# Reordering the first stage of a planned attention and feed-forward kernel: due times of its own for each of the first twelve f-tiles

## The chip, the cores and the metric

The kernel runs on one core of one Trainium2 chip. The metric is device time in microseconds of one execution; the median of several runs counts. Engines are named as in the profile: PE is TensorE, PEld its weight loads, DVE is VectorE, ACT is ScalarE, POOL is GpSimd, SP is SyncE, which issues most of the transfers.

## What is computed

Eight batches of eight heads of attention over 576 tokens with a head width of 64, and a feed-forward block of width 2048 on the result:

```python
scores = (q @ k.T) / sqrt(64)          # heads 0-3: only the last 32 keys
                                       # heads 4-7: only keys at a distance that is a multiple of 32
attn = exp(scores - max); attn /= sum(attn) + 1e-9
x = (attn @ v), heads side by side     # 4608 tokens x 512
h = x @ w_in                           # 512 x 2048
g = h * erf(softplus(h))
out = g @ w_out                        # 2048 x 512, float32
```

## The kernel before

**The work.** A pair of heads is one unit of attention; batch b has the pairs 0 to 3, and a name such as `qk_0_2` or `s_2_0` carries batch and pair. A pair goes through loads of qk and v, scores (PE), maximum, difference, exp and sum (DVE and ACT), the norm (POOL), a transposition, the product with v (PE), and a split of the result into a rounded part `xhi` (ACT, line 543) and a rest `xlo` (DVE, line 548). Batches 0 and 1 are written by `heads` (PE transposes, lines 505 and 524); batches 2 to 7 by `Pair` and `burst`, where one PE burst holds the product of one pair and the scores of the next (lines 649 and 669).

**Weights.** The feed-forward weights come as 64-bit words in sixteen tiles of 1 MB: w0 to w7 are pieces of `w_in`, w8 to w15 of `w_out`. `weight` unpacks each on DVE with three instructions (`bits0`, `bits1`, `bits2`, lines 849, 856, 862), rounds it on ACT (`split_hi`, line 867) and takes the rest on DVE (`split_lo_w`, line 870); the result is the tile `pair`.

**f-tiles.** `ftile` number k works on 128 columns of the hidden layer for 512 tokens of a batch: mm1 is twelve matmuls into a bank h or c (line 900); softplus and erf on ACT (lines 908, 911); the product on DVE (914); a rounded part `ghi` on ACT (917) and a rest `glo` on DVE (920); mm2 is twelve matmuls into the banks o0 to o3 (line 953). Two consecutive f-tiles share a tile of each weight. There are 144. Of the first, k = 0 to 3 are columns 0 to 3 of batch 0, k = 4 to 9 columns 0 to 5 of batch 1, k = 10 to 21 the others of batch 0. From k = 16 on mm1 uses the bank h alone, and a copy on DVE (`hs`, line 905) empties it.

**What sets the order.** Nothing is ordered by hand. `Plan` takes every step with an engine, an estimated duration, the steps it waits for and a due time, and lays the steps out one by one; the program is then written in that order, which each engine and each queue keeps. The due times are numbers in tables: KP for the attention pairs, KW for the unpacking of weights and KL for their loads, KI for the identity matrix, and FT for an f-tile: `at(i)` adds FT[i] to `PRO + SLOT * k` for softplus, erf, product, ghi, glo and mm2. `stash` stores the last 64 tokens of x on SP's queue for a chunk that is done at the end. Where PE would have nothing to do, the plan puts in a filler, a matmul of constants into a free bank (`warm`, line 1111), up to the mm1 of f-tile 6. `stay` (line 748) is four copies on POOL in a `Pair`; `PAIRS` says which banks and which weight tiles' room the pairs of batches 0 and 1 use.

Of the kernel before, what the change touches and what calls it, by code (L numbers as in the profile page):

```python
# [18 lines left out]
P = 128  # L19
# [9 lines left out]
PRO = 32  # L29
SLOT = 6.1  # L30
BACKLOG = 1.1130116
FT = (-2658.81, -1917.57, -3180.58, -1587.7, 370.28, 2216.13)
KI = -5711.28
KW = (
    (515.126, 145.354, -2348.96, -944.277, 1286.67, 3206.16, 5188.84, 898.14),
    (3223.92, 1696.94, 1126.17, 225.88, 917.373, 2507.48, 968.087, 687.694),
)
KL = (
    (1396.48, 770.086, 437.181, 1627.04, 1025.57, 3014.12, 4245.01, 2397.07),
    (945.031, -1252, 3215.3, 3000.01, 1806.83, 496.124, 738.615, -241.399),  # L40
)
KP = (
    (542.197, -1847.5, -1823.21, -1021.52, -228.67, -599.586, 241.152),
    (-276.384, -1335.88, 230.421, 74.7754, 61.6955, 1875.1, 500.521),
    (-3437.85, -358.658, -2301.53, -516.546, -1428.1, -1124.22, -1341.66),
    (-681.281, -64.094, -3.54274, 242.205, 753.958, -909.211, 891.395),
    (295.78, 1348.87, -519.101, -887.072, -1312.65, -1072.32, 546.505),
    (2178.78, -52.1175, 1285.12, 2385.15, -1099.07, 1937.66, 1486.77),
    (229.525, -1120.81, -1531.76, 458.111, -1237.4, 1489.49, 2057.23),
    (797.817, 454.351, -1337.33, -438.439, 405.282, -2692.97, -46.1439),  # L50
    (-263.256, -1479.86, -803.403, -1222.11, -1640.52, -729.701, -1160.22),
    (-56.753, -688.408, -1119, -2398.06, -1589.54, -528.693, -1803.55),
    (1701.86, -255.027, -218.21, 579.17, -2586.31, 474.53, 1124.51),
    (-1172.45, -389.859, -1119.5, 318.434, -1231.62, -605.957, 902.288),
    (2032.67, -285.494, 2320.84, 2718.33, 797.304, 1224.77, 2105.28),
    (185.837, 739.768, -248.587, 1446.15, 465.44, -982.033, -1572.57),
    (2173.08, -714.7, -89.7886, 1415.69, -653.201, 472.77, 2089.39),
    (-2448.89, -2823.79, -164.701, -2885.72, -3171.85, -833.514, -516.643),
    (173.604, -1291.81, 1443.08, 358.408, 1375.5, 281.827, 532.185),
    (-860.33, 173.881, -1669.94, -1368.01, -1271.17, -59.054, 19.7547),  # L60
    (-535.718, 791.315, -703.505, 428.52, -239.186, 1515.88, -829.14),
    (384.84, 22.9069, 191.935, 6.45996, 1625.85, 711.713, -785.021),
    (528.925, 813.537, -227.9, 758.411, 1271.32, -177.238, -283.018),
    (-983.339, 288.565, -1751.94, -152.244, -1780.28, -2884.66, -147.489),
    (-636.401, 555.939, -914.57, -54.0228, -991.538, -550.356, -1882.44),
    (-16.9022, -1698.68, -2124.61, -849.243, -749.766, -1907.47, 43.8626),
    (-281.424, 1163.73, 2667.33, 323.962, 2162.26, 1855.22, 2704.8),
    (-852.152, 81.5048, 131.859, -85.8376, 448.274, 857.394, -841.094),
    (1090.46, -1203.43, -1500.89, -1488.65, -582.704, -1479.82, -2024.72),
    (-1250.03, -2543.42, -1893.9, -2382.58, 212.636, -378.546, -1317.93),  # L70
    (-268.103, -1245.63, 369.011, -959.82, -353.937, -241.546, -491.086),
    (1006.02, -817.882, -1149.69, -1072.6, -81.8383, 825.626, 339.559),
    (614.205, 1964.07, 594.824, 1636.03, -61.9141, -185.064, 2530.02),
    (-444.459, -1478.15, -205.633, -1936.09, -288.964, -2805.35, -2230.9),
)
PAIRS = (
    (("h", "c"), None, True, True),
    (("o0", "o1"), (2, 3), True, True),
    (None, (10, 11), False, True),
    (("o2", "o3"), (4, 5), True, True),  # L80
    (None, (12, 13), False, True),
    (("o0", "o1"), (6, 7), True, True),
    (("o2", "o3"), (14, 15), True, True),
    (None, None, False, True),
)
# [79 lines left out]
class Plan:  # L165
# [114 lines left out]
def attention_moe(  # L280
# [329 lines left out]
    class Pair:  # L610
# [72 lines left out]
        def soft(self):  # L683
            loc, units, add = self.loc, self.units, plan.add
            cols = 64 * units
            k_q, k_v, k_s, k_m, k_n, k_t, k_x = self.keys
            s, pid = self.s, self.pid
            sm = buf("apool", "sm", [P, 2, 384], f"sm_{pid}")
            tt = buf("apool", "sm", [P, 2, 384], f"tt_{pid}")
            pt = buf("apool", "sm", [P, 2, 64 * units], f"pt_{pid}")  # L690
# [59 lines left out]
            def exchange():  # L750
# [4 lines left out]
            n = 2 * cols  # L755
            o = add("dve", dve(n), k_m, mask, [self.o_s], [], [s])
            o = add("dve", dve(n), k_m + 0.05, maxi, [o], [mx], [s])
            o = add("dve", dve(n), k_m + 0.1, less, [o], [sm], [s, mx])
            o = add("act", act(n, 0.08), k_m + 0.1, exp, [o], [], [sm])
            o.table = "exp"  # L760
            o = add("dve", dve(n), k_n, total, [o], [rc], [sm])
            o = add("dve", 0.31, k_n + 0.05, invert, [o], [], [rc])
            o = add("pool", 0.1 + n / 500.0, k_n + 0.1, norm, [o], [], [sm, rc])
            o = o_t = add("dve", dve(n) + 0.07, k_t, flip, [o, *turn_of("t")], [tt], [sm])
            turns["t"] = o
            o = add("pool", 0.0, k_t + 0.1, claim, [o], [pt])
            self.ready = [
                add("pool", 4 * (0.06 + cols / 1000.0), k_t + 0.2, stay, [o], [], [tt, pt]),
                add("sp", 1.0, k_t + 0.2, exchange, [o], [], [tt, pt]),
            ]  # L770
            self.ready[1].issues = 4
# [114 lines left out]
    def ftile(k, c, f, first_f, last_f, ready):  # L886

        v0 = PRO + SLOT * k
# [33 lines left out]
        add = plan.add  # L922
        ta, tp, td = act(CH), act(CH, 0.05), dve(CH)

        def at(i):
            return FT[i] + v0

        first = add("pe", 2.73, v0, mm1, ready[0] + mm1_first[-1:], [ph])
        first.words = 24
        o = first  # L930
        if not early:
            o = add("dve", td, at(2), keep, [o], [hs], [ph])
        o = add("act", tp, at(0), softplus, [o] + gates[-1:] * (k % 2 == 0), [a], [hs])
# [11 lines left out]
        for t in range(NTT):  # L945
# [4 lines left out]
            def mm2(t=t, po=po):  # L950
# [14 lines left out]
            if f == last_f:  # L965
# [25 lines left out]
                if t % 2 == 0:  # L991
                    o = o_e = add("act", act(DM, 0.06), v0 + 2.5 * SLOT + 0.7 + 0.2 * t, evac, [o], [ob], [po])
                else:
                    eng, n = ("dve", dve(DM)) if c == B else ("act", act(DM, 0.06))
                    o = add(eng, n, v0 + 2.5 * SLOT + 0.7 + 0.2 * t, evac, [o, o_e], [], [po, ob])
# [6 lines left out]
                else:  # L1002
                    o = add("pool", 1.2, o.key + 0.1, accumulate, [o, stored[c, t]], [], [ob])
# [25 lines left out]
    mm1_of, mm1_first, hi_of, gates = {}, [], [], []  # L1029
# [38 lines left out]
    for b in range(B):  # L1068
        p2 = b // 2
        for i, hp in enumerate(ORDER if p2 else (0, 1, 2, 3)):  # L1070
            keys = KP[4 * b + i]
            if p2 == 0:
                banks, home, act_sum, pool_norm = PAIRS[4 * b + i]
                done, o_s, o, loads = heads(
                    b, hp, keys, [], pe_mask=True, pool_norm=pool_norm, act_sum=act_sum, banks=banks, home=home, own=True
                )
# [11 lines left out]
            if p2:  # L1088
                n = 4 * b + i + 1
# [15 lines left out]
            chunk(B, 0, NFC)  # L1105
    def warm(tag):
        n = len(plan.ops)
        w = buf("ps_a", "ps", [P, 2, 512], f"warm{n}") if tag == "ps" else buf("ps_o", tag, [P, 512], f"warm{n}")

        def run():  # L1110
            yield nc.tensor.matmul(w[:, 0, :] if tag == "ps" else w[:, :], ident_b, con[:, :512], start=True, stop=True)

        return w, run

    w, run = warm("o3")
    first = plan.add("pe", 0.217, -10.0, run, o_con, [w])
    plan.filler = (first, warm, ("o3", "o2", "o1", "o0", "ps"), mm1_first[6])
    for op in plan.order():
        for x in op.new:
            x.tile = x.make()  # L1120
# [104 lines left out]
```

## Time and profile before

| | us |
|---|---|
| median of 3 runs | 910.86 (910.26 to 910.88) |
| the profiled execution, its own time | 910.45 |
| its span, first to last instruction | 908.7 |
| PE busy in the span | 874.5 |
| ACT busy | 588.5 |
| DVE busy | 500.2 |
| POOL busy | 116.1 |

The profile's page gives each engine's busy time and, in 40 slices of 22.7 us, its busy share in tenths. The chain of work is followed back from the last instruction: what released each step. A row of a timeline is start and duration in us, engine, line, operation, tile written and tile read; a number at the end in brackets is the idle time before it and what ended it. A busy PE is not PE at its peak, since the ends of its pipelined matmuls are modelled.

### The profile page before, as it was taken

The page shows a single profiled execution, that of the slowest core. Times are in us where ns is not written, and L with a number is a line of the kernel's source. Part 1 is how long each engine was busy: PE and PEld are TensorE (multiplying, and loading weights), DVE is VectorE, ACT ScalarE, POOL GpSimd, SP SyncE. Part 2 cuts the span into 40 slices and gives each one's busy share as a digit, 9 for nine tenths or more (in the row PEclk, how much of TensorE's full clock was granted, in tenths as well). Part 3 has the DMA queues.
Part 4 walks back from the last instruction along what each step waited for, and adds up shares of the span by engine and source line. Part 5 has one row for each costly group of instructions (what it writes and reads, how often), then busy time and mean ns, then how long its engine had stood idle before and what let it go on. Part 6 is the DMA issues. An engine that isn't in the chain of part 4 may idle for free.

```text
span 908.7 us, 18092 instructions
## 1 busy us (share of the span) xinstructions
PE 874.5 (96%) x7425; PEld 718.4 (79%) x7427; DVE 500.2 (55%) x793; ACT 588.5 (65%) x880; POOL 116.1 (13%) x156
## 2 busy tenths in 40 slices
PE   3678999999999999999999999999999999999997
PEld 2567888888888888888888888888888888888886
DVE  4998893555655545555555556555555333333332
ACT  2795876657666666677777667666766665556553
POOL 1210200021121111111111211111111100000000
PEclk9898999999999999999999999999999999999999
DMA  9995110133242122311221123212321310001001
GB/s 355 350 392 168 53 47 1 46 90 71 85 102 72 53 67 81 99 55 55 64 89 59 42 70 103 70 58 69 103 70 30 96 47 1 1 1 47 1 1 46
DMA packets 37298, 75.24 MB, mean 83 GB/s; under 512 B 12960, under 2 KB 16288, under 8 KB 37216
## 3 DMA queue, kind: packets, MB, share of 16 engines
q1 hardware_dynamic: 34576, 69.24, 22.5%
q0 software_dynamic: 2400, 4.46, 2.5%
q8 instruction: 58, 0.95, 0.4%
q10 hardware_dynamic: 240, 0.39, 0.2%
q14 instruction: 24, 0.20, 0.1%
HBM read 56.12 MB, written 13.63 MB: 77 GB/s over the span
## 4 chain that ended last, share of the span: by engine, by line
PE 92%; DVE 4%; ACT 2%; DMA 1%; issue 1%; SPq 0%; POOL 0%; DVEq 0%; ACTq 0%; POOLq 0%
PE o L953 44%; PE h L900 42%; PE x L669 3%; PE s L649 2%; ACT v L470 1%; DMA con<-consts 1%; DVE pair L870 1%; PE s L524 0%; DVE mx L434 0%; DVE w L856 0%; DVE w L862 0%; DVE w L849 0%; PE s L505 0%; DVE xlo L548 0%; DVE a L914 0%
## 5 line engine op out<-in xcount | busy, mean ns | idle before, releaser
L953 PE MATMUL o<-pair,ghi 128*128 128x512 f32 x1152 | 359.8, 394 | 2.6 <-DVE xlo L548 2.6
L900 PE MATMUL h<-xhi,pair 128*128 128x512 f32 x1152 | 287.0, 391 | 2.3 <-DVE a L914 2.1
L900 PEld LDWEIGHTS h<-xhi,pair 128*128 128x128 f32 x1152 | 216.6, 189 | 49.2 <-DVE a L914 2.4
L953 PEld LDWEIGHTS o<-pair,ghi 128*128 128x128 f32 x1152 | 215.2, 189 | 48.1 <-DVE xlo L548 2.7
L953 PE MATMUL o<-pair,glo 128*128 128x512 f32 x576 | 224.9, 391 | 0.0
L905 DVE COPY hs<-h 128x512 f32<-128x512 f32 x128 | 88.0, 688 | 158.6 <-PE h L900 158.6
L917 ACT CAST ghi<-a 128x512 fp32r<-128x512 f32 x144 | 89.1, 620 | 132.9 <-PE o L953 121.0
L900 PE MATMUL h<-xlo,pair 128*128 128x512 f32 x576 | 154.0, 389 | 0.0
L908 ACT ACTIVATE a<-hs 128x512 f32<-128x512 f32 x128 | 80.9, 632 | 99.1 <-DVE hs L905 84.7
L914 DVE TENSOR_TENSOR a<-a,hs 128x512 f32<-128x512 f32 x128 | 85.3, 708 | 102.1 <-ACT a L911 102.0
L920 DVE TENSOR_TENSOR glo<-a,ghi 128x512 fp32r<-128x512 f32 x144 | 99.3, 692 | 59.0 <-ACT ghi L917 58.0
L953 PEld LDWEIGHTS o<-pair,glo 128*128 128x128 f32 x576 | 108.7, 189 | 22.9
L900 PEld LDWEIGHTS h<-xlo,pair 128*128 128x128 f32 x576 | 108.1, 188 | 22.5
L908 ACT ACT_TABLE_LOAD x79 | 101.4, 1283 | 21.2 <-DVE hs L905 17.7
L726 POOL TENSOR_TENSOR sm<-sm,r 128x640 f32<-128x640 f32 (+1 forms) x24 | 36.3, 1513 | 470.3 <-DVE r L723 451.8
L911 ACT ACT_TABLE_LOAD x72 | 92.4, 1283 | 1.3
L911 ACT ACTIVATE a<-a 128x512 f32<-128x512 f32 x144 | 83.2, 624 | 0.8
L748 POOL COPY pt<-tt 32x320 f32<-32x320 f32 (+1 forms) x96 | 53.1, 553 | 39.5 <-DVE tt L732 36.0
L706 DVE TENSOR_TENSOR s<-s,con 128x640 f32<-128x640 f32 (+1 forms) x24 | 21.6, 900 | 31.6 <-PE s L649 31.6
L974 ACT COPY ob<-o 128x512 f32<-128x512 f32 x42 | 24.2, 585 | 10.9 <-PE o L953 8.6
L669 PEld LDWEIGHTS x<-pt,v 64*64 64x64 f32 x1392 | 24.4, 134 | 8.5 <-issue 8.5
L715 ACT ACT_TABLE_LOAD x24 | 30.8, 1283 | 0.4
(66 smaller groups left out, 503.1 us busy)
## 6 DMA issues: line engine op xcount, KB each, us to landing
v<-v_loc SPq DMA_DIRECT2D x16, 640.0 KB, 5.8
qk<-qk_loc SPq DMA_DIRECT2D x16, 592.0 KB, 5.5
words<-w_out SPq DMA_DIRECT2D x8, 1024.0 KB, 7.8
words<-w_in SPq DMA_DIRECT2D x8, 1024.0 KB, 7.3
out<-ob SPq DMA_DIRECT2D x32, 256.0 KB, 2.2
qk<-qk_res SPq DMA_DIRECT2D x12, 656.0 KB, 4.4
v<-v_str SPq DMA_DIRECT2D x16, 384.0 KB, 3.9
qk<-qk_str SPq DMA_DIRECT2D x4, 608.0 KB, 7.1
```

Of the source, the lines that this page charges most:

```text
L669: yield nc.tensor.matmul(self.x[m][d, n * a : n * (a + 1)], self.v[rows, (2 * a + h) * D : (2 * a + h) * D + D], p, start=True, stop=True,)
L715: yield nc.scalar.activation(sm[:, :, :cols], sm[:, :, :cols], AF.Exp, scale=1.0 / D**0.5)
L726: yield nc.gpsimd.tensor_tensor(out=wide(sm), in0=wide(sm), in1=spread(rc), op=ALU.mult)
L748: yield nc.gpsimd.tensor_copy(pt[quarter(m, f), f, :], plane(m, f, f))
L900: yield nc.tensor.matmul(ph[:, :CH], win[f // 2][:, w, 2 * P * cc + f0 : 2 * P * cc + f0 + P], x[cc][:, c0 : c0 + CH], start=(i == 0), sto ...
L905: yield nc.vector.tensor_copy(hs.tile, ph.tile)
L908: yield nc.scalar.activation(a.tile, hs.tile, AF.Softplus)
L911: yield nc.scalar.activation(a.tile, a.tile, AF.Erf)
L914: yield nc.vector.tensor_tensor(out=a.tile, in0=a.tile, in1=hs.tile, op=ALU.mult)
L917: yield nc.scalar.copy(ghi.tile, a.tile)
L920: yield nc.vector.tensor_tensor(out=glo.tile, in0=a.tile, in1=ghi.tile.bitcast(F32), op=ALU.subtract)
L953: yield nc.tensor.matmul(po.tile, g[:, ts], wout[f // 2][:, w, f % 2 * SW : f % 2 * SW + SW], start=(f == first_f and i == 0), stop=(f == ...
```

## The change

No step is added to the attention or the feed-forward work and none is taken away. What changes is the numbers by which the plan orders them, and four small things:

- a new table FE gives each of the first twelve f-tiles six due times of its own; FT, now with other numbers, holds from the thirteenth on
- KI, KW, KL and KP have other numbers throughout
- the plan's estimate of `stay` is 0.95 + cols/320 instead of 4 * (0.06 + cols/1000)
- fillers may use the banks c and h too, and go on up to the mm1 of f-tile 8
- PAIRS is written on one line, with the same content

```diff
-FT = (-2658.81, -1917.57, -3180.58, -1587.7, 370.28, 2216.13)
-KI = -5711.28
+FT = (-1281.04, -3645.45, -2381.23, -1076.53, 664.202, 2244.2)
+FE = (
+    (1750.73, -78.9746, -156.706, 86.3883, 561.264, -292.723),
...
+)
+KI = -1253.92
...
-                add("pool", 4 * (0.06 + cols / 1000.0), k_t + 0.2, stay, [o], [], [tt, pt]),
+                add("pool", 0.95 + cols / 320.0, k_t + 0.2, stay, [o], [], [tt, pt]),
...
-            return FT[i] + v0
+            return (FE[k][i] if k < len(FE) else FT[i]) + v0
...
-        w = buf("ps_a", "ps", [P, 2, 512], f"warm{n}") if tag == "ps" else buf("ps_o", tag, [P, 512], f"warm{n}")
+        if tag == "ps":
+            w = buf("ps_a", "ps", [P, 2, 512], f"warm{n}")
+        else:
+            w = buf("ps_h" if tag in "hc" else "ps_o", tag, [P, 512], f"warm{n}")
...
-    plan.filler = (first, warm, ("o3", "o2", "o1", "o0", "ps"), mm1_first[6])
+    plan.filler = (first, warm, ("o3", "o2", "o1", "o0", "ps", "c", "h"), mm1_first[8])
```

The new lines move the code: line 849 of before is 856 after, 914 is 921, 706 is 713, and so on by 7 (the filler, 1111, by 10).

SP's queue at the program's start, before. `ident` and `con` are constants, `words9` is a weight tile, `qk` and `v` the inputs of a pair.

```order
L1013 DMA ident_87<-ident_f 128x128
L384 DMA qk_0_2_89<-qk_str 128x1216
L838 DMA words9_93<-w_out 128x2x1024
L384 DMA qk_0_3_95<-qk_str 128x1216
L387 DMA v_0_2_90<-v_str 128x768
L384 DMA qk_0_1_99<-qk_loc 128x1184
L1010 DMA con_85<-consts 128x576
L387 DMA v_0_3_96<-v_str 128x768
L384 DMA qk_1_2_108<-qk_str 128x1216
L384 DMA qk_1_0_113<-qk_loc 128x1184
L387 DMA v_0_1_100<-v_loc 128x1280
L387 DMA v_1_2_109<-v_str 128x768
```

The same place after.

```order
L391 DMA qk_0_0_87<-qk_loc 128x1184
L1020 DMA ident_90<-ident_f 128x128
L391 DMA qk_0_2_92<-qk_str 128x1216
L1017 DMA con_85<-consts 128x576
L391 DMA qk_0_1_96<-qk_loc 128x1184
L394 DMA v_0_0_99<-v_loc 128x1280
L394 DMA v_0_2_93<-v_str 128x768
L391 DMA qk_0_3_147<-qk_str 128x1216
L394 DMA v_0_1_97<-v_loc 128x1280
L845 DMA words8_240<-w_out 128x2x1024
L845 DMA words0_288<-w_in 128x4x512
L391 DMA qk_1_2_311<-qk_str 128x1216
```

The first weight goes from the third place to the tenth, the constants from the seventh to the fourth, pair 0 of batch 0 to the front.

DVE around the mask of `s_2_0`, its first instruction of batch 2, before. `w32` and `pair` are weight tiles being unpacked, `a` and `glo` belong to f-tiles.

```order
L849 TENSOR_SCALAR w32_15_1079<-words15_994 128x1024
L920 TENSOR_TENSOR glo_2_1085<-a_2_1004,ghi_2_1077 128x512
L548 TENSOR_TENSOR xlo3_84<-s_1_3_784,xhi3_80 128x18x18
L548 TENSOR_TENSOR xlo3_84<-s_1_3_784,xhi3_80 128x18x14
L856 SCALAR_TENSOR_TENSOR w32_15_1079<-words15_994,w32_15_1079 128x1024
L862 SCALAR_TENSOR_TENSOR w32_15_1079<-words15_994,w32_15_1079 128x1024
L706 TENSOR_TENSOR s_2_0_1098<-s_2_0_1098,con_85 128x2x320
```

The same place after.

```order
L856 TENSOR_SCALAR w32_2_1055<-words2_958 128x1024
L555 TENSOR_TENSOR xlo0_81<-s_1_0_859,xhi0_77 128x256
L555 TENSOR_TENSOR xlo0_81<-s_1_0_859,xhi0_77 128x320
L863 SCALAR_TENSOR_TENSOR w32_2_1055<-words2_958,w32_2_1055 128x1024
L869 SCALAR_TENSOR_TENSOR w32_2_1055<-words2_958,w32_2_1055 128x1024
L927 TENSOR_TENSOR glo_3_1127<-a_3_971,ghi_3_1124 128x512
L713 TENSOR_TENSOR s_2_0_1083<-s_2_0_1083,con_85 128x2x320
```

Before, the unpacking ahead of the mask covers w9, w1, w8, w0, w2, w3, w11, w7 and w15, the last two without `split_lo_w`; after it covers w8, w0, w1, w9, w4 and w2, again the last two without it. The mask is DVE's instruction 113 before (counted from 0, the branch at the start among them) and 101 after.

## Rows read from the trace of the kernel before

**Rows 1.** The page: busy us (share) xinstructions; below, busy tenths in 40 slices.

```profile
PE 874.5 (96%) x7425; PEld 718.4 (79%) x7427; DVE 500.2 (55%) x793; ACT 588.5 (65%) x880; POOL 116.1 (13%) x156
...
PE   3678999999999999999999999999999999999997
...
DVE  4998893555655545555555556555555333333332
```

**Rows 2.** The chain (start us, us, what), and PE's only wait after 84 us.

```profile
84.48 5.71 PE h L900 x24
...
152.78 2.72 PE h L900 x12
...
PE h L900 <- DVE hs L905: 0.2, 1, 0.2
```

**Rows 3.** Stretches: us, busy by engine (x instructions), PE's granted clock, DMA share, GB/s.

```profile
7.97:84.52 76.55, 54.38 (x1146) 41.95 (x1148) 67.69 (x112) 51.40 (x165) 13.79 (x13) 0.87 0.92 339
84.52:137.10 52.58, 52.58 (x232) 43.48 (x233) 46.84 (x56) 41.45 (x54) 5.01 (x5) 1.00 0.16 57
137.10:151.45 14.35, 14.35 (x65) 11.89 (x64) 4.58 (x8) 7.97 (x12) 0.00 (x0) 1.00 0.00 1
```

**Rows 4.** Timeline of DVE, the mask of `s_2_0`.

```profile
84.52 0.83 DVE L706 TENSOR_TENSOR s<-s,con 128x640 f32<-128x640 f32 x1
```

**Rows 5.** Unpacking on DVE, 7.97 to 84.52 us: ns min/median/max, first and last start.

```profile
L849 DVE TENSOR_SCALAR w<-words x9: 655/694/1954, 8.0 to 79.5; 128x1024 uint32<-128x1024 uint32 x9
L856 DVE SCALAR_TENSOR_TENSOR w<-words,w x9: 1209/1226/1773, 8.7 to 82.1; 128x1024 uint32<-128x1024 uint32 x9
L862 DVE SCALAR_TENSOR_TENSOR w<-words,w x9: 1211/1225/1744, 10.0 to 83.3; 128x1024 uint32<-128x1024 uint32 x9
L870 DVE TENSOR_TENSOR pair<-w,pair x7: 1185/1217/1226, 12.3 to 68.8; 128x1024 fp32r<-128x1024 f32 x7
```

**Rows 6.** The start: DVE's first instruction, the constants and PE in the chain, DVE's first reduce.

```profile
7.97 0.69 DVE L849 TENSOR_SCALAR w<-words 128x1024 uint32<-128x1024 uint32 x1 [7.97 <-DMA words<-w_out]
...
4.01 8.37 DMA con<-consts
12.43 0.82 PE s L411 x2
...
13.44 0.95 DVE L434 TENSOR_REDUCE mx<-s 128x12 f32<-128x768 f32 x1
```

**Rows 7.** Transfers issued by 24 us: queue, count, KB each, median us to landing.

```profile
qk<-qk_str SPq DMA_DIRECT2D x4, 608.0 KB, 7.1
words<-w_out SPq DMA_DIRECT2D x2, 1024.0 KB, 10.2
...
qk<-qk_loc SPq DMA_DIRECT2D x3, 592.0 KB, 10.9
v<-v_str SPq DMA_DIRECT2D x3, 384.0 KB, 8.8
...
con<-consts SPq DMA_DIRECT2D x1, 144.0 KB, 8.4
ident<-ident_f SPq DMA_DIRECT2D x1, 64.0 KB, 1.8
```

**Rows 8.** Stretches up to the landing of the constants, columns as in rows 3.

```profile
0.00:4.00 4.00, 0.00 (x0) 0.00 (x0) 0.00 (x0) 1.49 (x2) 0.30 (x5) 1.00 0.44 132
4.00:12.38 8.38, 1.56 (x48) 1.37 (x48) 3.23 (x4) 1.04 (x1) 0.00 (x0) 1.00 1.02 406
```

**Rows 9.** Timeline of PE, a filler.

```profile
37.37 0.63 PE L1111 MATMUL warm<-con 128*128 128x512 bf16 x1
```

**Rows 10.** Timeline of SP, the first store of rest tokens.

```profile
26.00 0.33 SPq L1051 DMA_DIRECT2D rests<-xhi  x1
```

**Rows 11.** Timeline of POOL and DVE, a norm and an unpacking step that it overlaps.

```profile
55.61 2.17 POOL L496 TENSOR_TENSOR v<-v,r 128x384 f32<-128x384 f32 x2 [5.70 <-DVE r L488]
...
57.09 1.77 DVE L856 SCALAR_TENSOR_TENSOR w<-words,w 128x1024 uint32<-128x1024 uint32 x1
```

More of the change, by code (lines that the diff above doesn't have):

```diff
@@ L31 @@
 BACKLOG = 1.1130116
-FT = (-2658.81, -1917.57, -3180.58, -1587.7, 370.28, 2216.13)
-KI = -5711.28
+FT = (-1281.04, -3645.45, -2381.23, -1076.53, 664.202, 2244.2)
+FE = (
+    (1750.73, -78.9746, -156.706, 86.3883, 561.264, -292.723),
+    (-1873.53, -1131.49, -3255.33, -1932.5, -68.3526, -2636.75),
+    (-440.156, 494.33, -2418.01, -324.007, -279.52, -1957.1),
+    (-2493.93, -2196.69, -1337.47, -2683.09, -1942.8, -740.706),
+    (-359.715, -339.561, -756.812, -395.038, -948.712, 554.973),
+    (-1263.5, 98.006, -351.554, -2365.23, -1954.63, -1761.8),
+    (-241.219, -1177.42, 1412.51, 536.763, 444.719, -1139.03),
+    (644.806, -259.744, 2143.44, 1710.4, 45.7892, -1067.48),
+    (-1711.86, -1443.44, -2327.25, -3586.51, -1397.29, 33.4301),
+    (3.46292, -743.115, 1066.95, 192.768, 1894.77, -563.446),
+    (1907.55, 232.81, 1702.22, 1883.28, 1449.51, 1639.92),
+    (251.398, 289.473, 1152.01, 183.239, 186.521, 2052.03),
+)
@@ L34 @@
+KI = -1253.92
 KW = (
-    (515.126, 145.354, -2348.96, -944.277, 1286.67, 3206.16, 5188.84, 898.14),
-    (3223.92, 1696.94, 1126.17, 225.88, 917.373, 2507.48, 968.087, 687.694),
+    (859.316, -364.277, 1752.25, 515.707, 1791.43, 2209.92, 3085.75, 3085.77),
+    (964.206, 1279.48, 376.87, 2481.16, 2013.31, 1647.44, 1824, 2823.4),
 )
 KL = (
-    (1396.48, 770.086, 437.181, 1627.04, 1025.57, 3014.12, 4245.01, 2397.07),
-    (945.031, -1252, 3215.3, 3000.01, 1806.83, 496.124, 738.615, -241.399),
+    (480.387, 1288.46, 2416.18, 3375.64, 122.711, 140.933, 815.996, 2353.63),
+    (472.202, 1803.57, 3101.11, 2412.69, 1077.94, 891.415, 2540.97, 1971.9),
@@ L41 @@
 )
 KP = (
[L43 to L74, printed above, removed]
-)
[L76 to L85, printed above, removed]
+    (-2410.44, -565.175, -748.178, 438.18, -1080.03, -2885.02, -1037.93),
@@ new lines @@
+    (102.959, -1193.73, 70.9719, 3287.5, 455.664, -892.601, 840.696),
+    (-900.525, -782.133, 405.097, -810.419, 734.34, -16.3521, 1098.34),
+    (143.076, 1011.45, -2590.86, 1010.92, -3292.49, 1029.15, -1216.39),
+    (789.018, 1048.65, -714.381, 626.825, -922.112, -2306.85, -1465.63),
+    (559.553, -729.782, 225.212, -774.318, 844.792, -1322.87, 775.077),
+    (496.835, 77.9573, 1467.81, 218.702, -1077.89, -224.7, -1005.89),
+    (726.325, 906.548, -1714.7, -469.763, -2746.43, 336.621, -625.5),
@@ new lines @@
+    (1336.3, -1856.27, -1256.05, -679.77, 568.949, -2415.03, -798.584),
+    (714.022, -1045.07, -2962.96, -1469.33, -1971.2, -1376.3, -2291.13),
+    (314.077, -1263.28, -2056.91, -451.032, -5164.66, -22.9832, -2584.5),
+    (-2168.42, -1681.23, -1838.99, -1593.33, -2784.94, -3409.02, -3118.26),
+    (2065.3, -275.204, 1934.09, 2662.4, -140.127, 1458.16, 328.273),
+    (-977.492, 1203.22, -1002.34, -258.98, 869.831, -1890.54, -2300.62),
+    (1819.99, -732.235, -5.44976, 728.019, 520.445, 1148.26, 2261.54),
@@ new lines @@
+    (-2647.96, -3519.98, 2.83719, -3759.74, -3996.15, -2116.22, -1267.97),
+    (823.491, -1497.27, 791.163, -33.3544, 1698.3, 1218.39, 98.8672),
+    (-32.2775, 675.893, -144.183, -410.41, -598.029, -775.023, 302.519),
+    (564.453, 1093.16, 68.9, 397.763, 334.012, 2686.61, 39.4621),
+    (-118.704, -529.226, -564.076, -123.487, 1260.35, 2043.96, -1547.74),
+    (-761.339, -132.305, -807.645, 122.702, 460.693, -1188.03, -426.413),
+    (-1478.45, 332.134, -1756.26, -38.1205, -1664.99, -3031.01, -1251.64),
@@ new lines @@
+    (40.6675, 1863.57, -2.41413, -781.475, -54.737, -598.267, -834.709),
+    (1150.33, -2887.39, -1156.47, -657.281, -868.561, -2532.62, -720.501),
+    (-15.0147, 429.842, 2166.7, -628.703, 2564.97, 1763.7, 1664.59),
+    (-2831.2, 671.269, 549.714, -727.477, -150.019, 567.778, -792.61),
+    (165.722, -2198.62, -2886.16, -2477.69, -787.532, -1956.78, -1847.81),
+    (-2800.82, -3775.29, -3349.52, -4684.04, -1217.21, -1309.54, -2782.29),
+    (-926.989, -1998.65, 1040.37, -848.821, -63.1487, -759.522, -686.435),
@@ new lines @@
+    (458.849, -1314.35, -2417.41, -503.189, 524.657, -374.027, 1279.35),
+    (-440.039, 2898.77, 668.055, 1975.17, 300.075, -1082.98, 1119.07),
+    (-50.2768, -448.019, -804.848, -764.196, 310.162, -2270.43, -2440.03),
+)
+PAIRS = ((("h", "c"), None, True, True), (("o0", "o1"), (2, 3), True, True), (None, (10, 11), False, True), (("o2", "o3"), (4, 5), True, True), (None, (12, 13), False, True), (("o0", "o1"), (6, 7), True, True), (("o2", "o3"), (14, 15), True, True), (None, None, False, True))
```

## The prediction

> **What bounds the kernel now.** I read three views in this order. First the page's busy times and its slices: TensorE is busy 96% of the span, and its row reads 9 from the fifth slice on, while VectorE reads 8 or 9 in slices two to six and mostly 5 later [rows 1]. So the kernel has two regimes. Second the chain and TensorE's waits: from 84.48 us, where mm1 of f-tile 4 starts, TensorE works without a break and waits 0.2 us in all until the end [rows 2]. What follows 84.48 is a fixed amount of matmul work, and the change neither adds nor removes any of it: both orders hold the same matmuls after the scores of batch 2 (tile `s_2_0`). So the time can move by the moment at which TensorE reaches `s_2_0`, and by stalls that come after it. Third the engines in that first regime: between 7.97 and 84.52 us VectorE is busy 67.69 of 76.55 us, TensorE 54.38, ScalarE 51.40 [rows 3]. VectorE is the bound there; its waits are 76.55 - 67.69 = 8.9 us. The mark on VectorE is the mask of `s_2_0`, its first instruction of batch 2, at 84.52 [rows 4].
>
> **VectorE ahead of the mark.** The order shows what stands ahead of the mask in the two programs. The softmax, the x splits, the products and the three glo's are the same in number. Of the unpacking of weights (`bits0`, `bits1`, `bits2`, `split_lo_w`), before has 9, 9, 9 and 7 instructions there, after 6, 6, 6 and 4: the unpacking of three weight tiles is moved behind the mark. By the medians [rows 5] one of each is 0.694 + 1.226 + 1.225 + 1.217 = 4.36 us, so 13.1 us leave the bound engine; 67.69 - 13.1 = 54.6 us stay.
>
> **The start.** VectorE now fills its first wait with weight 9, which landed at 7.97; the first softmax runs at 13.44, behind the constants, which were issued at 4.01 and took 8.37 us [rows 6]. They stand seventh on SP's queue, behind 3,280 KB; with their own 144 KB that is 3.51 MB [rows 7]. The windows say 0.53 MB moved by 4.00 us and 406 GB/s after that [rows 8], so 3.51 MB were through at 11.3 and the landing came 1.0 us later, at 12.38. After, they stand fourth, behind qk_0_0 (592), ident (64) and qk_0_2 (608): 1,408 KB or 1.44 MB with their own, through at 4 + (1.44 - 0.53)/0.406 = 6.2, landed at 7.3. The mask matmuls take 0.82 and VectorE starts 0.2 later, so at 8.3 instead of 7.97: nearly the same start, now with softmax and not with a weight. The weights 8 and 0 then stand tenth and eleventh (5.4 and 6.5 MB, so 17 and 19.6 us by the same sum); VectorE has seventeen short softmax instructions in front of them.
>
> **The waits.** Nothing in the trace shows how long VectorE will wait in the new order, so it gets bounds. If the waits stay as they are (8.9), the mask is at 8.3 + 54.6 + 8.9 = 71.8, which is 12.7 us earlier. Upper bound: the 4.4 us that weight 9 filled become a wait as well, 13.3 in all, 8.3 us earlier. Lower bound: 4 us, less than half of today's, 17.6 us earlier; TensorE allows little more, since it has 54.38 us of work in that stretch itself. I take the middle, as the orders alternate softmax and weights in like manner.
>
> **What is late next.** The unpacking is not gone, it now lies behind the mark, where TensorE never waits today because VectorE is busy only 46.84 of 52.58 us and then 4.58 of 14.35 [rows 3]. The first place at which TensorE needs VectorE with all weights done is f-tile 17: its mm1 takes the h bank that the copy `hs_16` (line 905) empties. Today mm1 of f-tile 17 starts at 152.78 [rows 2], 68.3 us after the mask; the new order has three more matmuls in between (0.7 us), so 68.9. Ahead of the copy VectorE will have 46.84 + 4.58 = 51.4, plus 13.1, less one `split_lo_w` that is put behind it (1.2): 63.3 us; with the copy itself (0.7) and today's waits until 137.1 (52.58 - 46.84 = 5.7) it is done at 69.7 against 68.9: a stall of 0.8 to 0.9 us. Bounds: no wait, no stall; twice the waits, 6.6 us. I take 0.9, because an engine that runs behind its suppliers waits less, not more. The weights themselves are in time: w10 begins six instructions behind the mask and is first needed by f-tile 8's mm2, 168 matmuls of 0.227 us (2.72 for twelve [rows 2]) or 38 us behind `s_2_0`, and by the same count w3, w11, w6 and w7 stand earlier in VectorE's order than TensorE asks for them.
>
> **Edits with no term.** Eleven more filler matmuls (14 for 3) of 0.63 us [rows 9] stand where TensorE idles, 76.55 - 54.38 = 22 us of it [rows 3]; without that cover the five just ahead of mm1 of f-tile 0 could cost 3 us, and if they keep the clock up they give some back (0.87 granted in that stretch, 1.00 after). The new duration of `stay` (line 748) only moves the plan. `PAIRS` is unchanged in content. Batches 2 to 7 keep their distance between bursts to within some us, and the end holds the same work.
>
> **Sum.** 12.7 - 0.9 = 11.8 us. The profiled execution took 910.45 us (span 908.7 and 1.8 around it), the median of the runs is 910.86, 0.4 above. 910.45 - 11.8 + 0.4 = 899.1.
>
> **Rivals.** (1) *Half the gain*: waits of 13.3 us at the start and a stall of 3 at f-tile 17: 8.3 - 3 = 5, so 905.9. For it: the early softmax waits for ScalarE's long exp_sum rows, and nothing fills them. Against: VectorE has the next head to work on.
> (2) *More*: waits of 4 us, fillers that hold the clock, no stall: some 16, so 894.9. For it: the granted clock was 0.87 in the stretch [rows 3]. Against: TensorE's own 54.38 us.
> (3) *It doesn't do it*: the mask comes earlier but the stall at f-tile 17 takes all back, because VectorE's load up to there is the same and only its waits can shrink; about 910.9. For it: the forecast needs VectorE busy for 118.6 (54.6 + 63.3 + 0.7) of 132.7 us, 89%; at 82%, 118.6 of the 144.5 us from 8.3 to 152.8, nothing is left. Against: while it had work it was 88% busy in the first stretch and 89% in the second [rows 3].
> (4) *Slower, by SP's queue*: SP works in order. Today the first store of rest tokens (`stash`) is issued at 26.00 [rows 10], with three weight loads ahead of it; after, it is SP's seventeenth instruction, waits for the last split of the first head, and fourteen of the sixteen weights are queued behind it. Each us that this head is late makes w1 and all later weights a us late. With 12.6 MB up to and including w1 it lands at 34.8 if the queue never runs dry; VectorE wants it after 52 of the 101 instructions ahead of the mask, by that share from about 35 us on. So it decides from a delay of a few us, and with VectorE dry for 13 us the time would be 910.9 + 13 - 11.8 = 912.1. For it: in-order waits; against: the split is VectorE's 29th instruction, due at some 24 us.
> (5) *Slower, by the port*: while GpSimd's 2.17 us norm ran at 55.61, a `bits1` took 1.77 instead of 1.23 [rows 11]; over the stretch the unpacking cost 3.2 us above its medians against 13.79 us of GpSimd work. If all GpSimd time of both stretches (13.79 + 5.01 = 18.8 [rows 3]) came out of VectorE, 15.6 us more, the time would be 914.7. The Trainium skill (SBUF — State Buffer, section "SBUF: two separate sides") states such a lock: of VectorE's two-input instructions and GpSimd's, the one that starts first holds the port pair for its whole length. The trace agrees with blocking, but at 3.2 of 13.79 us; the order puts no more GpSimd work beside VectorE than there was.
>
> **How the numbers follow.** Chances: forecast 0.55, (1) 0.18, (2) 0.12, (3) 0.07, (4) 0.05, (5) 0.03. Between 893.5 and 906.5 lie the forecast, (1) and (2), 0.85 of it, less their edges. About 0.2% (1.8 us) is what a measurement of this kernel can tell from no change. Faster by more than that: 0.85; within: 0.07; slower: 0.08.
>
> **What would show it.** The mask of `s_2_0` on VectorE at 69 to 75 us, mm1 of f-tile 4 just behind it, TensorE's row at 8 or 9 in the fourth slice and 9 from then on. First VectorE reduce near 8.3, constants landed near 7.3. A single wait of TensorE for `hs` near f-tile 17, of about a us. I am wrong if the mask stays behind 80, if `bits0` of w1 waits for its load, or if TensorE waits for glo or pair tiles between f-tiles 8 and 20.

## The result

The changed kernel takes 898.28 us (median of four runs, 895.70 to 900.85) against 910.81 us before: a ratio of 0.9864, 95% interval 0.9835 to 0.9892. Run again in a second comparison it took 900.05 us, ratio 0.9882 (0.9866 to 0.9897). The forecast of 899.1 us lies between the two medians. The profiled execution of the change took 895.70 us with a span of 893.9; it was the fastest of all its runs, which matters below.

The page of the changed kernel, lines that answer to [rows 1], with TensorE's granted clock by slices:

```profile
PE 874.7 (98%) x7434; PEld 718.0 (80%) x7438; DVE 500.3 (56%) x793; ACT 584.9 (65%) x878; POOL 118.3 (13%) x156
...
PE   6989999999999999999999999999999999999997
...
DVE  5899994555555455555555545565546333333332
...
PEclk9899999999999999999999999999999999999999
```

TensorE's busy time is the same (874.5 before), its share is larger: its row reads 9 from the fourth slice on instead of the fifth. The two stretches of the changed kernel, split at VectorE's first reduce, at the mask of `s_2_0` and at the copy `hs_16` (columns as in [rows 3]):

```profile
7.92:69.38 61.46, 54.55 (x1125) 42.12 (x1128) 54.93 (x101) 48.55 (x163) 15.58 (x13) 0.89 1.00 368
69.38:136.38 67.00, 67.00 (x297) 55.33 (x296) 63.74 (x74) 51.93 (x68) 5.54 (x5) 1.00 0.26 95
```

VectorE's three marks in its timeline (lines are 7 further down than before):

```profile
7.92 0.89 DVE L441 TENSOR_REDUCE mx<-s 128x5 f32<-128x320 f32 x2 [7.92 <-PE s L418]
...
37.97 0.71 DVE L856 TENSOR_SCALAR w<-words 128x1024 uint32<-128x1024 uint32 x1 [0.70 <-DMA words<-w_in]
...
69.38 0.83 DVE L713 TENSOR_TENSOR s<-s,con 128x640 f32<-128x640 f32 x1
```

The chain around the mask, and all that TensorE waits for behind it:

```profile
64.70 2.94 PE o L960 x12
67.65 0.97 PE s L656 x64
68.61 5.71 PE h L907 x24
```

```profile
PE h L907 <- DVE xlo L824: 0.6, 2, 0.4
PE o L960 <- ACT ob L981: 0.2, 1, 0.2
```

The mask is at 69.38 instead of 84.52 [rows 4], 15.1 us earlier, and the span is 14.8 us shorter. From the mask to the end it is 824.2 us before and 824.5 after. So all of the gain was made ahead of the mask, as forecast. TensorE's first mm1, before and after, divides it further:

```profile
47.62 2.15 PE L900 MATMUL h<-xhi,pair 128*128 128x512 f32 x8
```

```profile
34.86 2.21 PE L907 MATMUL h<-xhi,pair 128*128 128x512 f32 x8
```

That is 12.8 us earlier, so 12.8 of the 15.1 us lie ahead of the first mm1. From 8 us to there VectorE has 22.5 us of work instead of 33.7, and TensorE 23.6 instead of 24.3, at a granted clock of 0.81 instead of 0.87; from there to the mask VectorE has 32.3 instead of 34.0. The question for the experiments is what brings this.

### The profile page after: what moved, and what is told of

It reads as the page before. It is cut to its first block, busy times and chain, and to the rows that moved or that the text cites. A ratio compares the mean times of both kernels' runs of the same rounds, so it can differ in the third digit from the quotient of the medians.

```text
span 893.9 us, 18113 instructions
## 1 busy us (share of the span) xinstructions
PE 874.7 (98%) x7434; PEld 718.0 (80%) x7438; DVE 500.3 (56%) x793; ACT 584.9 (65%) x878; POOL 118.3 (13%) x156
## 4 chain that ended last, share of the span: by engine, by line
PE 93%; DMA 2%; ACT 2%; DVE 1%; issue 1%; SPq 0%; DVEq 0%; ACTq 0%
PE h L907 44%; PE o L960 43%; PE x L676 3%; PE s L656 2%; DMA words<-w_in 1%; PE s L531 1%; DMA qk<-qk_str 1%; ACT L918 0%; ACT v L477 0%; DMA v<-v_str 0%; DVE a L921 0%; ACT a L918 0%; PE s L512 0%; DVE pair L877 0%; ACT a L915 0%
## 5 line engine op out<-in xcount | busy, mean ns | idle before, releaser
L960 PE MATMUL o<-pair,ghi 128*128 128x512 f32 x1152 | 358.1, 392 | 0.2 <-ACT ob L981 0.2
L960 PEld LDWEIGHTS o<-pair,ghi 128*128 128x128 f32 x1152 | 214.1, 188 | 46.1 <-ACT ob L981 0.6
L960 PE MATMUL o<-pair,glo 128*128 128x512 f32 x576 | 224.2, 389 | 0.0
L960 PEld LDWEIGHTS o<-pair,glo 128*128 128x128 f32 x576 | 108.1, 188 | 22.6
L907 PEld LDWEIGHTS h<-xlo,pair 128*128 128x128 f32 x576 | 108.1, 188 | 22.5
L739 DVE STREAM_TRANSPOSE tt<-sm 128x320 f32<-128x320 f32 (+1 forms) x48 | 23.2, 521 | 10.7 <-POOL sm L733 10.6
```

The costliest lines, as they stand in the source:

```text
L907: yield nc.tensor.matmul(ph[:, :CH], win[f // 2][:, w, 2 * P * cc + f0 : 2 * P * cc + f0 + P], x[cc][:, c0 : c0 + CH], start=(i == 0), sto ...
L960: yield nc.tensor.matmul(po.tile, g[:, ts], wout[f // 2][:, w, f % 2 * SW : f % 2 * SW + SW], start=(f == first_f and i == 0), stop=(f == ...
```

## The experiments

One table first. "To the end" is the profiled span less the start of the mask of `s_2_0`. Ratios are to the kernel before on the same chip.

| kernel | median us | ratio, 95% interval | mask at | to the end |
|---|---|---|---|---|
| before | 910.81 | | 84.52 | 824.2 |
| changed | 898.28 | 0.9864, 0.9835 to 0.9892 | 69.38 | 824.5 |
| changed, again | 900.05 | 0.9882, 0.9866 to 0.9897 | 72.70 | 825.9 |
| changed, one filler | 901.78 | 0.9895, 0.9875 to 0.9916 | 72.69 | 824.9 |
| changed, + 7.4 us VectorE ahead | 904.97 | 0.9936, 0.9921 to 0.9951 | 77.40 | 825.2 |
| changed, + 7.4 us VectorE behind | 905.85 | 0.9951, 0.9932 to 0.9970 | 71.59 | 830.8 |
| changed, constants late | 904.65 | 0.9917, 0.9894 to 0.9940 | 77.96 | 825.7 |
| changed, four more fillers | 903.21 | 0.9910, 0.9895 to 0.9925 | 73.81 | 827.6 |
| changed, without FE | 913.29 | 1.0027, 1.0013 to 1.0040 | 69.89 | 839.6 |
| before, three weights behind | 930.51 | 1.0206, 1.0187 to 1.0225 | 85.89 | 843.7 |
| before, early start | 910.93 | 0.9997, 0.9988 to 1.0006 | 84.87 | 824.5 |
| before, both | 930.66 | 1.0212, 1.0198 to 1.0227 | 85.98 | 843.4 |
| before, 12.3 us less VectorE | 910.62 | 0.9991, 0.9977 to 1.0005 | 83.78 | 823.5 |
| before, batch 0 first | 917.94 | 1.0085, 1.0067 to 1.0103 | 91.69 | 823.6 |

In ten of the fourteen the last column is 823.5 to 827.6: what follows the mask costs the same as long as nothing stalls there. The other four are the runs in which something does. The last two columns are read from one execution each.

**The change again.** Nothing altered.

> The changed kernel, nothing altered, for the spread of its runs and a second profile. Its first four runs lay between 895.7 and 900.9 us, and the spans went with the mean granted clock (0.992 with 893.9, 0.988 with 899.1). Theory: ahead of the mask of s_2_0 VectorE (54.9 of 61.5 us) and TensorE (54.6) are now nearly level, so the time depends on how long TensorE stands at its lower clock there; then the median is 896 to 901, the mask moves between about 69 and 75 us from profile to profile, and a later mask goes with a lower granted clock ahead of it. Rival: the spread comes from somewhere behind the mask; then the mask stays at 69.4 within 0.5 us whatever the time of the run is.

Median 900.05, 899.09 to 900.93. The mask was at 72.70, 3.3 us later than in the first profile. Stretches of this profile: the first 8 us, and from there to the mask:

```profile
0.00:8.00 8.00, 1.41 (x80) 1.16 (x80) 0.00 (x0) 1.49 (x2) 0.30 (x5) 1.00 0.74 226
...
8.00:72.70 64.70, 56.99 (x1127) 43.61 (x1128) 55.27 (x100) 48.75 (x163) 15.86 (x13) 0.84 0.98 357
```

The same in the first profile of the change:

```profile
0.00:8.00 8.00, 1.97 (x82) 1.45 (x83) 0.07 (x1) 1.49 (x2) 0.30 (x5) 1.00 0.79 268
...
8.00:69.38 61.38, 54.47 (x1125) 42.12 (x1128) 54.86 (x101) 48.55 (x163) 15.58 (x13) 0.89 1.00 368
```

The transfers moved 226 instead of 268 GB/s in the first 8 us, and VectorE's first reduce came at 9.20 instead of 7.92. Then the same matmuls took TensorE 57.0 instead of 54.5 us, with 0.84 granted instead of 0.89; the chain has the last mm2 ahead of `s_2_0` as `67.09 4.54 PE o L960 x12`, where it was 2.94. So the theory fits: a later mask goes with a lower granted clock. Of the 3.3 us, 1.3 are there at VectorE's first reduce; that the clock makes the rest is read from these two profiles, not tested. VectorE's work is 55 us in both. The 895.7 us of the first profile is the low end of what this program takes, not its usual time.

**One filler.** All but the first of the 14 left out:

```diff
+    steps = [o for o in steps if o is first or o.words != 2 or o.eng != "pe"]
```

> The changed kernel with the first filler alone; the other 13 fillers, matmuls of 0.6 us that feed nothing, are left out. Theory A (they stand where TensorE idles anyway, and VectorE sets the mask of s_2_0): same time, within 2 us of 898.3, mask at 69 to 70. Theory B (they keep the clock up, and TensorE is level with VectorE by now): a lower granted clock ahead of the mask, mask 2 to 6 us later, 900 to 904. Theory C (they cost time, since the ones just ahead of the first mm1 delay it): 2 to 6 us faster, 892 to 896.

901.78 us, 897.68 to 903.61, and the mask at 72.69, where it was in the second profile with all fillers. The intervals of the two ratios overlap: no effect is shown, and one of up to some 3 us isn't excluded.

**More work on VectorE, ahead of the mask and behind it.** `bits1` and `bits2` issued twice for three weights (in the second run the weights are 3, 13, 12):

```diff
+        if o.weight in (1, 9, 4) and name in ("bits1", "bits2"):
+            o.emit = twice(o.emit)
```

> The changed kernel with the bits1 and bits2 steps of weights w1, w9 and w4 issued twice (the second time writes the same values again): 6 x 1.23 = 7.4 us more work on VectorE ahead of the mask of s_2_0. Theory (VectorE is the bound ahead of the mask, and each us of its work there is a us of the time): mask at 75.5 to 77, time 6 to 7.4 us longer, 904 to 906. Rival (with TensorE now at 54.6 of the 61.5 us it bounds the stretch, and VectorE fits beside it): 0 to 4 us longer.

> The changed kernel with the bits1 and bits2 steps of weights w3, w13 and w12 issued twice: the same 7.4 us more on VectorE, but behind the mask of s_2_0. Theory (behind the mask TensorE sets the pace and VectorE has room: 63.7 us of work in 67.0 us until the copy hs_16, and mm1 of f-tile 17 does not wait for that copy now): the mask stays at 69 to 70, the wait for hs is 0 to 4 us, the time 0 to 4 us longer, 898 to 902. Rival (the work is on the path wherever it stands, so that moving three weights could not have brought anything by itself): 6 to 7.4 us longer, 904 to 906.

Ahead: 904.97, 4.9 us over the 900.05 of the change on the same chip, with the mask 4.7 later; of 7.4 us 2.5 found room. That lies between the two expectations of 6 to 7.4 and 0 to 4. The chain now is VectorE's, through the doubled steps, up to the mm2 ahead of `s_2_0`:

```profile
66.01 2.17 DVE w L863
...
68.21 1.24 DVE w L869
...
69.47 1.22 DVE w L869
...
71.29 0.42 DVE xlo L555
...
71.75 4.57 PE o L964 x12
```

Behind: 905.85, 5.8 us more. Here my theory (0 to 4) missed, and the rival's 6 to 7.4 came near. TensorE's waits behind the mask, and the longest in its timeline:

```profile
PE h L911 <- DVE a L925: 3.1, 3, 2.1
```

```profile
107.31 3.53 PE L911 MATMUL h<-xhi,pair 128*128 128x512 f32 x8 [2.11 <-DVE a L925]
```

mm1 waits for the product that empties its bank, which stands in VectorE's queue behind an unpacking. The eight matmuls after that wait then took 3.53 us where they take 2.09 elsewhere, so 3.1 us of waits cost 4.9 us (830.8 to the end against 825.9). VectorE had little room on either side of the mask: the new order is nearly level, not relieved.

**The three weights alone.** In the kernel before:

```diff
+    behind = steps[steps.index(unpacking(6)[-1]) + 1]
+    move(11, unpacking(13)[0])
+    move(7, behind)
+    move(15, behind)
```

> The kernel before, with one thing of the change alone: the unpacking of three weights is moved behind the mask of s_2_0 (w11 ahead of w13, w7 and w15 behind w6); loads, start, fillers and all else stay as before. Theory V (VectorE's work ahead of the mask is what set the mask): the mask comes 9 to 13 us earlier, at 71.5 to 75.5, and the time is 898 to 902. Theory T (ahead of the mask TensorE and VectorE were nearly level in the kernel before as well; TensorE was busy without a break from 73.2 to 84.5 at a granted clock of 0.56 to 0.58, so only that low clock and the last waits go): 4 to 7 us, 904 to 907. If the weights are not the cause at all: 909 to 912.

930.51: none of the three expectations. The mask in VectorE's timeline, and TensorE's waits behind it:

```profile
85.89 0.83 DVE L706 TENSOR_TENSOR s<-s,con 128x640 f32<-128x640 f32 x1 [3.91 <-PE s L649]
```

```profile
PE h L904 <- DVE a L918: 14.6, 2, 9.8
```

Two things at once. VectorE was done early and stood 3.9 us waiting for TensorE's scores: the mask had another reason to be where it was. A part of that may be TensorE's clock: 0.80 granted from 8 us to the mask, where the kernel before had 0.87, and 57.4 us for the matmuls that took 54.4 there. (The 0.56 to 0.58 of the expectation held from 72 to 80 us only; from 80 to 84 it was 1.00.) And three unpackings put where nobody had made room cost 14.6 us of waits behind it.

**The start alone, and both.** Constants right behind `qk_0_2`; w9 between the softmax steps:

```diff
+    steps.remove(o_con[0])
+    steps.insert(steps.index(loads[1]) + 1, o_con[0])
+    w9 = [o for o in steps if o.weight == 9 and o.eng != "sp"]
...
+    at = steps.index(sums[1])
+    steps[at:at] = w9[:2]
```

> The kernel before, with the other part alone: the constants' load is put right behind that of qk_0_2, and w9 is unpacked between the first softmax steps instead of ahead of them. First reduce on VectorE at 7 to 8.5 instead of 13.4. Theory V (VectorE's sum of work ahead of the mask is the same 67.7 us, and only the order in it changes): the mask moves by less than 2 us, time 909 to 912. Rival S (the early softmax starts everything earlier by the 5 us): the mask at 79 to 81, time 905 to 907.

> The kernel before with both parts: three weights' unpacking moved behind the mask, and the earlier constants with w9 between the softmax steps. Theory V: as with the weights alone, within 2 us of it. Rival S: the gain of the weights alone and some 5 us more. If the two together come to 898 to 901, they are the whole of what the change brings, without its new due times and its other orders; if they stay above 904, most of it comes from the order of batch 0 and 1, which they leave as before.

The start alone: 910.93, no difference. VectorE's timeline:

```profile
7.60 0.96 DVE L434 TENSOR_REDUCE mx<-s 128x12 f32<-128x768 f32 x1 [7.60 <-PE s L411]
...
84.87 0.83 DVE L706 TENSOR_TENSOR s<-s,con 128x640 f32<-128x640 f32 x1
```

The first softmax came 5.8 us earlier than in [rows 6] and the mask not at all. TensorE's first mm1 was not earlier either: 49.23 against 47.62. Both: 930.66, as the weights alone.

**Less work on VectorE, nothing moved.** The cleanest question to the kernel before: `bits1` and `bits2` of five weights left out.

```diff
+    steps = [o for o in steps if not (o.weight in (1, 8, 0, 2, 3) and o.emit.__name__ in ("bits1", "bits2"))]
```

> The kernel before with less work on VectorE and nothing moved: the bits1 and bits2 steps of five weights (w1, w8, w0, w2, w3) are left out, so those weights hold part of their bits only. That takes 10 x 1.23 = 12.3 us from VectorE between 24 and 62 us, ahead of the mask of s_2_0, and adds nothing behind it. Theory V (VectorE alone set the mask, as the chain has it from 40 to 73 us): the mask at 72 to 76, the time 898 to 902. Theory T (taking work from VectorE only uncovers the next chain, through ScalarE and TensorE at its low clock, as happened where three later weights were moved): the mask at 80 to 86, the time 906 to 912; between the two: each has a share.

910.62, ratio 0.9991: theory T. The stretch to the mask has 55.31 us of VectorE work instead of 67.7, and ends 0.7 us earlier. TensorE's granted clock in it was 0.80 instead of 0.87, and its work 56.7 us instead of 54.4, so some 2 us of the missing gain may be the clock's, which leaves more than 9 of the 12.3:

```profile
8.00:83.78 75.78, 56.68 (x1149) 43.81 (x1152) 55.31 (x103) 51.04 (x165) 13.57 (x13) 0.80 0.93 342
```

Its chain shows what stands behind VectorE's:

```profile
63.08 8.32 PE h L904 x24
71.41 0.86 PE s L524 x44
...
73.01 1.28 ACT L912
...
76.71 0.63 ACT a L915
77.34 0.69 ACT sm L511
...
78.08 0.91 PE s L524 x44
78.98 2.95 PE o L957 x12
81.93 0.97 PE s L649 x64
```

Two mm1 (8.32 us, 5.71 at the full clock), then ScalarE with the activations of f-tiles 2 and 3, then its copy of pair 1_3's probabilities, and only then that pair's product and the mm2. ScalarE keeps the written order, so the copy waits for the activations ahead of it: TensorE has its input ready at 76.2 us (`75.38 0.82 PE L505` in its timeline), and it starts at 77.34. In the changed kernel the copy stands ahead of those activations (`45.48 0.69 ACT sm L518` in its chain). But the last product ahead of `s_2_0` is there that of pair 1_0, and its copy in turn stands behind both softplus steps and one erf of f-tiles 2 and 3 (`62.58 0.71 ACT qk L518`): this way is still there, only earlier. In the kernel before, the way through TensorE and ScalarE was as long as the one through VectorE, at the clock of this run. VectorE's lesser work did not bring the first mm1 earlier either: it came at 49.27.

**The constants late**, in the changed kernel; four loads ahead of them:

```diff
+    loads = [o for o in steps if o.eng == "sp"]
...
+    steps[steps.index(o_con[0]) : steps.index(o_con[0])] = loads[4:8]
```

> The changed kernel with one thing undone at the start: four loads of batch 0 (qk_0_1, v_0_0, v_0_2, qk_0_3) are put ahead of the constants, which then stand eighth on SP's queue. By the bytes ahead of them the constants land at about 13 us instead of 7.4, and VectorE's first reduce moves from 8 to 9 to about 14. Theory V (VectorE has nothing else to do in the new order, and its work ahead of the mask is what counts): the mask 4 to 6 us later, time 903 to 906. Rival (the first weights and loads set the pace until 35 us, as the start moved in the kernel before had cost and brought nothing): less than 2 us.

904.65, 4.6 us over the 900.05 of the change; by the two ratios, 0.9917 and 0.9882, it is 3.2. VectorE's timeline:

```profile
15.46 0.89 DVE L441 TENSOR_REDUCE mx<-s 128x5 f32<-128x320 f32 x2 [15.46 <-PE s L418]
...
77.96 0.82 DVE L713 TENSOR_TENSOR s<-s,con 128x640 f32<-128x640 f32 x1
```

Against the second profile of the change the first reduce is 6.3 us later and the mask 5.3, though TensorE's clock was higher here (0.90 granted from 8 us to the mask, 0.84 there). The start that brought nothing in the old order is worth something in the new one: half to three quarters of its length by the medians, more by the mask.

**Without FE.** All f-tiles by FT:

```diff
-            return (FE[k][i] if k < len(FE) else FT[i]) + v0
+            return FT[i] + v0
```

> The changed kernel without the table FE: all f-tiles take their due times from FT, all other tables as in the change. The start, the first four f-tiles' mm1 and the six weights ahead of the mask of s_2_0 stay as they are; what differs is mm2 of the first f-tiles, some fillers and the order of the weights behind the mask. If the weights and the start carry the gain: within 2 us of the changed kernel, 897 to 902, mask at 69 to 74. If the order of the first f-tiles carries it: 4 us or more slower, with the mask later or with waits of TensorE behind it.

913.29: the whole gain is gone, but not ahead of the mask, which is at 69.89. It is lost behind. TensorE's stretches (us and busy us first) without FE, and in the change:

```profile
60.00:160.00 100.00, 95.76 (x559) 76.31 (x561) 80.22 (x98) 71.51 (x96) 7.51 (x6) 1.00 0.25 97
160.00:260.00 100.00, 97.70 (x991) 80.13 (x990) 57.25 (x93) 67.74 (x93) 22.18 (x28) 1.00 0.33 81
```

```profile
60.00:160.00 100.00, 98.37 (x651) 80.99 (x655) 82.70 (x100) 73.53 (x99) 6.68 (x6) 1.00 0.27 99
160.00:260.00 100.00, 99.84 (x976) 82.39 (x970) 58.42 (x96) 70.06 (x95) 23.15 (x29) 1.00 0.37 90
```

From 60 to 860 us TensorE is busy 797.5 us in the change and 788.9 here, 8.6 less. The plan lays the steps out one after the other, so a first f-tile that falls elsewhere moves all that follow. Another 6.4 us lie in TensorE's busy time itself (881.1 in all, 874.7 in the change). Of these 3.5 are fillers, thirteen on record behind the mask, where the change has none; they stand where TensorE would wait, as here, ahead of a wait for a product:

```profile
78.25 1.69 PE L1121 MATMUL warm<-con 128*128 128x512 bf16 x6
80.56 2.11 PE L907 MATMUL h<-xhi,pair 128*128 128x512 f32 x8 [0.63 <-DVE a L921]
```

So the waits are longer than the idle time shows. What makes the other 3 us is open.

**Four more fillers** in a wait of TensorE, for its clock:

```diff
+    gap = [o for o in steps if o.eng == "pe"][38]
+    x, keep_warm = warm("h")
+    at = steps.index(gap)
...
+    steps[at:at] = fill
```

> The changed kernel with four more filler matmuls on the bank h, in the 1.6 us in which TensorE waits for a copy ahead of the scores' product at 46.2 us; behind that wait f-tile 2's mm1 took 4.22 us in one profile and 4.54 in the next, against 2.77 at the full clock. Theory (the clock fell because TensorE stood still there, and TensorE is on the path by now): that mm1 takes 2.77 to 3.2, the mask comes 1 to 2 us earlier than without, time 1 to 2 us shorter than the changed kernel on the same chip. Rival (the clock has fallen for something earlier, or the time so won is lost again at the next wait): mm1 as before or the mask unmoved, time within 0.7 us; if the fillers themselves delay the product, up to 1 us slower.

903.21, 3.2 us over the change, or 2.5 by the ratios: a miss. TensorE's timeline:

```profile
47.71 1.30 PE L1121 MATMUL warm<-con 128*128 128x512 bf16 x3 [2.22 <-DVE a L921]
```

The bank h was not free when I took it to be: the fillers waited for the product that empties it, and the pair's product behind them started at 48.94 instead of 46.22 (in the first profile of the change, whose first mm1 was 0.9 us earlier). The mm1 after them still took 3.57 us. This run shows the price of a filler on a bank in use, and decides nothing about the clock.

**Batch 0 first**, in the kernel before: by then TensorE had reached `s_2_0` 33 to 37 us after its first mm1 in most runs, and I took the end of batch 0's attention for the cause. The edit also makes w0 and w1 change places, puts batch 1's first pair and w1's unpacking further back, and leaves out the fillers but the first.

```diff
+    head = [o_ident, q[0, 2], o_con[0], q[0, 1], q[0, 0], q[0, 3], v[0, 2], v[0, 1], v[0, 0], v[0, 3], load[0], load[9]]
+    queue["sp"] = head + [o for o in queue["sp"] if o not in head]
...
+    put_at("dve", early, inv[1])
+    put_at("dve", third, inv[2], 1)
...
+    put_at("pe", late, mm1_first[1], 1)
```

> The kernel before with batch 0 put first, by hand: its qk and v loads and the constants stand ahead of all weights and of batch 1 on SP's queue, w0 and w1 change places, pair 0_0's softmax runs ahead of 0_3's, no weight is unpacked ahead of batch 0's maxima, and batch 1's first pair and w1's unpacking come behind batch 0's x. All nine weights stay ahead of the mask of s_2_0. In the runs so far TensorE reached s_2_0 33 to 37 us (40 with more work on VectorE) after the first mm1, whatever stood between, with that mm1 at 47.6 to 50 us in the kernel before and its variants and at 35 to 37 in the changed kernel, 42 with its constants late. Theory F (the end of batch 0's attention sets the mask): first mm1 at 37 to 42, s_2_0 at 71 to 78, time 898 to 904. Theory V (the 67.7 us of VectorE ahead of the mask bound it once the start is early): first mm1 as early, but the mask not before 79, 904 to 909; then both, the order and the three weights, are needed. Neither: mask at 83 or later, 908 or more.

917.94, slower; the case called "neither". The first mm1 came at 43.58, 4.0 us earlier than the 47.62 of the kernel before, and the mask at 91.69. The chain:

```profile
43.58 7.21 PE h L904 x24
...
74.48 0.82 DVE w L862
...
79.19 1.87 DVE w L849
81.06 0.34 DVE xlo L548
...
81.45 2.93 PE o L957 x6
```

From 57 to 81 us it runs through VectorE, one unpacking after the other. So the distance of 33 to 37 us was no law, and that theory falls too. TensorE's clock was 0.73 from 8 us to the mask. Even so, the first mm1 is 8.7 us later than in the changed kernel: this order by hand is not the order of the change.

## Why the prediction was right, point by point

**The time came out, by the right arithmetic for the new order.** For the profiled execution I had 898.65 us; it took 895.70. The 3.0 us between are 2.4 from the mask (71.8 forecast, 69.38), 0.9 from a stall that didn't come, less 0.3 behind. Term by term: the start 8.3, measured 7.92; VectorE's work 54.6, measured 54.93; its waits 8.9, measured 6.5. The waits were the mis-sized term, inside their bounds of 4 and 13.3. The same sum for the second profile: 9.20 of start, 55.3 of work, 8.2 of waits. So the match of the forecast with the medians has some luck in it: the low waits of the first profile and the later start of the second are both spread that the forecast had no term for.

**The bound was only half read.** The step "VectorE is the bound there" says more than its rows. In the new order it holds nearly: 7.4 us more work moved the mask by 4.7, and a start 6.3 us later moved it by 5.3. In the old order it does not: 12.3 us less work moved it by 0.7, the three weights moved away left it where it was, and so did the earlier start. Being busy for 67.69 of 76.55 us meant that the mask could not come much earlier without less work on VectorE. It did not mean that less work would bring it, since a second way through TensorE and ScalarE ended at the same time. The Trainium skill (Perfetto Trace Analysis, section "Identifying the Most-Contended Engine") says to optimize the engine of the highest occupancy first. VectorE had it, at 88% of the stretch, and the run with 12.3 us less of it measured 0.9991: followed alone, the rule would have brought nothing here. The change shortened both ways at once: up to the first mm1, 12.8 us earlier, VectorE has 11.1 us less work, and TensorE stands idle for 3.3 us instead of 15.3. The sum that I put on record had only VectorE's part of this. That the order of the same steps on ScalarE and TensorE was needed beside it is read from the chains; no run has that order alone in the kernel before, so it is argued, not shown. Nor was the order of batch 0 tried together with three weights less.

**Behind the mask** I said that the rest is fixed, and that 13.1 us more of VectorE would stall it by 0.9 us. There was no stall: VectorE had 63.74 us of work (63.3 forecast), and its waits were 3.3 instead of 5.7, so `hs_16` was done in time. But the room was as thin as that sum said. Another 7.4 us cost 4.9 us there, and three weights at places that had not been fitted for them 19.5. "In time by the count of matmuls" was too coarse a reason: what fails first is not the weight but the product that stands in VectorE's queue behind it.

**Edits with no term.** The fillers at nothing: not contradicted, not shown. That FE had no term was an omission: it carries the order behind the mask, and without it the time is 913.29.

**The rivals.** (1), half the gain, and (3), none, would have shown as longer waits and a stall: neither is there. (2), 894.9 us, came nearest to the profiled execution, and for part of its reason: waits of 6.5 us, no stall. (4), SP's queue: `bits0` of w1 did wait for its load, the sign I had named, but 0.70 us, under the few us from which it decides. (5), the port: GpSimd worked 15.58 us beside VectorE in the stretch, more than before, and VectorE's work came out 0.3 us above the forecast.

## What to carry to other kernels

The busiest engine of a stretch tells how early the stretch can end, not what ends it: before work is moved off that engine, leave some of it out in a trial run, since that costs one run and shows the next chain. When a second chain ends with the first, as the one through TensorE and ScalarE did here, look for a change of order that shortens both at once; each part of it alone may bring nothing, as the weights and the start did. Work that is moved "behind" needs its place between the products there as much as the work that was freed.

## What the runs showed of the hardware

A wait of TensorE can cost more than itself. After a wait of 2.11 us the next eight matmuls of mm1 took 3.53 us, where they take 2.09 at the full clock: TensorE had been busy without a break from 95 to 105 us at a granted clock of 1.00, and over these matmuls it was granted 0.55, which is near the lower of its two levels, 1.2 of 2.4 GHz. In the first profile of the change they took 3.37, behind waits of 1.57 and 0.26 us with the pair's product in between:

```profile
46.22 0.78 PE L531 MATMUL s<-sm,v 64*64 64x54 f32 x34 [1.57 <-ACT sm L518]
47.27 0.57 PE L531 MATMUL s<-sm,v 64*64 64x54 f32 x10 [0.26 <-issue]
47.77 3.37 PE L907 MATMUL h<-xhi,pair 128*128 128x512 f32 x8
```

It isn't the wait alone that decides: behind the same wait of 1.25 us (product of pair 1_0, ahead of mm2) the twelve matmuls took 2.94 us at a granted clock of 1.00 in one profile of the same program, and 4.54 at 0.63 in the next. And the same program's first transfers moved 268 GB/s over 8 us in one execution and 226 in another, in which VectorE's first instruction came 1.3 us later. Both bear on the spread of the changed kernel's runs, 5 us where those of the kernel before lay within 0.6 in the same comparison and 3.3 in the next; that they make all of it is not shown.
